# From a list scheduler to a written order with transposes on quarters of the array: a recurrent attention layer feeding a softplus layer

## The chip, the cores and the metric

The kernel runs on one core of one Trainium2 chip. The time is the device's own, in microseconds (us), for one execution. A profile is one execution recorded by the hardware profiler; its span is shorter than the timed median of the same kernel (345.8 against 349.65 us for the kernel before). TensorE is PE in the profile (PEld its weight loads), VectorE is DVE, ScalarE is ACT, GpSimd is POOL, SyncE is SP.

## The reference, cut to what matters

```python
for t in range(S):                       # S = 768, for 4 x 8 heads of 40
    y[:, :, t] = einsum('bhd,bhde->bhe', r_t, state)
    Sa = einsum('bhde,bhe->bhd', state, a_t)
    state = state * w_t - einsum('bhd,bhe->bhde', Sa, b_t) + einsum('bhd,bhe->bhde', v_t, k_t)
...                                      # y as x: 3072 tokens of 320
h = x @ w_in                             # 320 x 2048
g = maximum(h, 0) + log1p(exp(-abs(h)))
out = g @ w_out                          # 2048 x 320
```

The kernel cuts the 768 steps into 12 chunks of 64. Inside a chunk the recurrence becomes products of 64x64 (many, one per head), the inverse of a triangular matrix, and a state that passes from chunk to chunk. Two chunks share one inversion, called a window. The first two windows are inverted on VectorE, the other four on GpSimd, by an elimination of 60 steps.

## The kernel before

The program is a graph of 1839 operations. At build time a list scheduler gives each an engine, a place in the order and a PSUM bank. Each engine then takes its list in that order, waiting on semaphores (in the profile TensorE once stood 5.6 us before a product whose weights, `wout`, had not landed). Cut to what the argument touches:

```python
BLOCK, AHEAD, FETCH, BEFORE = 256, 82, 2300.0, 70    # its model of TensorE's instruction fetch
SLOW = ("h", "o", "csb")                             # dense-layer products, kept for the ends of lines
COUNT = {"tr": 8, "tot": 16, "gram": 32, ...}        # products per operation
...
def schedule(ops):
    ...
                pen = SWITCH if e == "pe" and mode is not None and o.mode != mode else 0.0
                if e == "pe":
                    pen += fetch.run(s + pen, c, 2 * COUNT[o.name])
                    if o.name in SLOW:
                        want = FILL if fetch.wants(s) else -SAVE
...
        def transpose(src, srcs, t, off):            # 72 of these, 8 products on the whole array each
            def f(e):
                for bp in X2:
                    for yy in range(H_ // 2):
                        i = T.transpose(pb(t)[:, bp, off + 128 * yy:off + 128 * yy + 128],
                                        src[:, bp, 128 * yy:128 * yy + 128], ident[:, :])
                return i
            return op(pe(8 * 56.0), srcs + ["ident"], [t], f, mode=FULL, name="tr")
...
        gexc = Ring("gexc", NEAR, [128, 2, DM], F32)  # NEAR = 4: chunk 5 takes the buffer of chunk 1
        nh = Ring("nh", NEAR, [128, 2, 512], BF)
```

Most of TensorE's products run on quarters of the array (64x64; 32 of them take 0.27 us in the trace, where a transpose of 8 products on the whole array takes 0.45). The transposes and the dense layers h and o run on the whole of it. A product is two TensorE instructions, a weight load and a matmul (8016 of each in the profile). The profile's instruction queue moved 63 packets of 16384 bytes, and 2 x 8016 instructions are 62.6 times 256. A "line" below is such a packet, or the 256 instructions that go with it.

## Time and profile before

| | before |
|---|---|
| time, 3 runs at first | 349.65 us (349.4 to 350.46) |
| span of the profile | 345.8 us |
| TensorE products, lines of 256 instructions fetched | 8016, 63 |
| first elimination step on GpSimd (the hand-over) | 114.7 us |
| end of the mask that closes GpSimd's last elimination | 294.3 us |
| from there to the end | 51.5 us |
| TensorE waits named "issue" | 4.1 us in 7 |

"GpSimd's steps" below means the time from the hand-over to the end of that mask. The three stages are a head up to the hand-over, GpSimd's chain of four inversions beside TensorE, and a tail. The page's chain of work that ended last, followed back from the end, with shares of the span by engine and then by line:

```profile
PE 47%; ACT 11%; POOL 9%; DMA 9%; SPq 9%; DVE 7%; issue 5%; ACTq 2%; DVEq 0%; POOLq 0%
PE ps L1205 12%; PE ps L1224 12%; SPq L664 8%; PE ps L730 7%; POOL mt L971 4%; DMA wout<-in_moe_w_out_dram 3%; POOL mtmp L967 3%; ACT gT L1214 3%; ACT et L1211 3%; PE ps L773 2%; DMA a_f<-in_a_dram 2%; PE ps L1073 2%; ACTq L664 2%; DMA r_f<-in_r_dram 2%; PE ps L1174 2%
```

TensorE holds 47% of the chain. "issue", time with nothing visible to wait for, has 5%. The kernel's own waits of that kind are these (engine, tile, line; total us, times, longest):

```profile
PE ps L832 <- issue: 1.7, 2, 1.0
...
PE ps L1073 <- issue: 1.4, 3, 0.7
...
PE ps L1050 <- issue: 0.5, 1, 0.5
PE ps L1174 <- issue: 0.5, 1, 0.5
```

They add up to 4.1 us.

### The profile page before, as it was taken

Reading aid. Unit: us, or ns where it says so; the run is one execution under the profiler, and the core shown is the slowest. Engines: PE = TensorE matmul, PEld = TensorE weight load, DVE = VectorE, ACT = ScalarE, POOL = GpSimd, SP = SyncE. Lnnn points to the kernel's source line nnn. Section 1 sums busy time; section 2 is a strip of 40 time slices with the busy share of each in tenths; the row PEclk is TensorE's granted clock in tenths of the full one; section 3 lists DMA queues with packets and bytes.
Section 4 is the critical chain, followed back from the end, with each engine's and each line's share of the span. In section 5 each row is a group of like instructions: output and inputs, shape, how many; then the busy total and the mean of one; then the engine's idle time right before and its main releaser. Section 6 shows DMA issues by size and latency. Waiting matters only on the chain.

```text
span 345.8 us, 17638 instructions
## 1 busy us (share of the span) xinstructions
PE 280.4 (81%) x8016; PEld 212.7 (61%) x8016; DVE 232.7 (67%) x419; ACT 210.3 (61%) x296; POOL 169.2 (49%) x309
## 2 busy tenths in 40 slices
PE   0337247688789969999799999998989899999873
PEld 0226126576567747777577776786766678777642
DVE  7729978889997746657756697585885656664201
ACT  1246704226797825877568888667687368667661
POOL 8106000001000627898888788898888888000000
PEclk9967865569999978999899999999999999999999
DMA  8999984687667565676546465430411400100101
GB/s 134 171 174 142 182 159 79 107 145 113 122 120 156 103 112 94 123 126 108 102 79 104 83 104 96 78 69 14 89 34 21 91 14 13 33 6 21 39 22 38
DMA packets 145787, 31.30 MB, mean 90 GB/s; under 512 B 140272, under 2 KB 145392, under 8 KB 145712
## 3 DMA queue, kind: packets, MB, share of 16 engines
q1 hardware_dynamic: 129504, 25.09, 42.9%
q10 hardware_dynamic: 13728, 2.46, 5.1%
q0 software_dynamic: 2480, 2.62, 4.7%
q8 instruction: 63, 1.03, 1.2%
q14 instruction: 12, 0.10, 0.1%
HBM read 28.84 MB, written 3.93 MB: 95 GB/s over the span
## 4 chain that ended last, share of the span: by engine, by line
PE 47%; ACT 11%; POOL 9%; DMA 9%; SPq 9%; DVE 7%; issue 5%; ACTq 2%; DVEq 0%; POOLq 0%
PE ps L1205 12%; PE ps L1224 12%; SPq L664 8%; PE ps L730 7%; POOL mt L971 4%; DMA wout<-in_moe_w_out_dram 3%; POOL mtmp L967 3%; ACT gT L1214 3%; ACT et L1211 3%; PE ps L773 2%; DMA a_f<-in_a_dram 2%; PE ps L1073 2%; ACTq L664 2%; DMA r_f<-in_r_dram 2%; PE ps L1174 2%
## 5 line engine op out<-in xcount | busy, mean ns | idle before, releaser
L1205 PE MATMUL ps<-xT,win 128*128 128x256 bf16 x576 | 79.9, 275 | 3.5 <-ACT et L1211 1.8
L1211 ACT ACTIVATE et<-ps 128x512 f32<-128x512 f32 x96 | 57.2, 596 | 36.3 <-PE ps L1205 35.8
L967 POOL TENSOR_TENSOR mtmp<-mt 128x30 f32<-128x30 f32 (+14 forms) x120 | 60.5, 504 | 33.0 <-DVE mt L960 24.3
L971 POOL TENSOR_TENSOR mt<-mt,mtmp 128x30 f32<-128x30 f32 (+14 forms) x120 | 66.8, 557 | 8.7
L1224 PE MATMUL ps<-wout,gT 128*128 128x320 bf16 x384 | 65.2, 302 | 5.9 <-ACT gT L1214 2.9
L1205 PEld LDWEIGHTS ps<-xT,win 128*128 128x128 bf16 x576 | 50.6, 98 | 15.9 <-ACT et L1211 6.0
L1214 ACT ACTIVATE gT<-et,hln 128x1024 bf16<-128x1024 f32 x48 | 55.2, 1151 | 1.4
L1224 PEld LDWEIGHTS ps<-wout,gT 128*128 128x128 bf16 x384 | 34.2, 98 | 20.1 <-ACT gT L1214 4.6
L1035 POOL CAST r_b<-r_f 128x640 bf16<-128x640 f32 x12 | 9.5, 789 | 44.2 <-DMA r_f<-in_r_dram 39.6
L1035 POOL CAST v_b<-v_f 128x640 bf16<-128x640 f32 x12 | 9.2, 765 | 37.0 <-DMA v_f<-in_v_dram 24.8
L1229 DVE TENSOR_TENSOR osb<-ps,csb 128x320 f32<-128x320 f32 x24 | 11.6, 484 | 20.3 <-PE ps L1224 20.1
L785 DVE TENSOR_TENSOR qt<-ps,sut 128x1024 bf16<-128x1024 f32 x12 | 14.6, 1221 | 5.6 <-PE ps L773 5.6
L814 PE MATMUL ps<-lw,nexc 64*64 64x320 bf16 x96 | 7.2, 361 | 13.8 <-ACT lw L845 13.6
L814 PE MATMUL ps<-lw,ninc 64*64 64x320 bf16 x96 | 9.8, 328 | 8.5 <-ACT ginv L862 6.2
L785 DVE TENSOR_TENSOR tak<-ps,sut 128x1024 bf16<-128x1024 f32 x12 | 14.6, 1219 | 2.8 <-PE ps L773 2.6
L785 DVE TENSOR_TENSOR pt<-ps,sut 128x1024 bf16<-128x1024 f32 x12 | 14.6, 1216 | 2.6 <-PE ps L773 2.6
L1180 DVE TENSOR_TENSOR yo<-ps,gexc 128x640 bf16<-128x640 f32 x12 | 9.9, 821 | 8.3 <-PE ps L1174 8.2
L845 ACT ACTIVATE lw<-w_f 128x1280 bf16<-128x1280 f32 x6 | 7.7, 1282 | 12.3 <-DMA w_f<-in_w_dram 12.3
L868 DVE TENSOR_TENSOR kh<-k_f,ginv 128x640 bf16<-128x640 f32 x12 | 10.9, 910 | 4.8 <-DMA k_f<-in_k_dram 4.8
L985 ACT ACTIVATE dex<-dc,blk 128x1024 bf16<-128x1024 bf16 x6 | 6.9, 1146 | 11.6 <-DVE dc L979 11.6
L866 DVE SCALAR_TENSOR_TENSOR nh<-b_f,ginv 128x640 bf16<-128x640 f32 x12 | 9.9, 825 | 5.3 <-ACT ginv L862 5.3
L862 ACT ACTIVATE ginv<-ps 128x640 f32<-128x640 f32 x12 | 8.4, 704 | 8.0 <-issue 6.8
(152 smaller groups left out, 587.9 us busy)
## 6 DMA issues: line engine op xcount, KB each, us to landing
out_dram<-osb SPq DMA_DIRECT2D x48, 80.0 KB, 2.3
b_f<-in_b_dram SPq DMA_DIRECT2D x44, 80.0 KB, 3.6
v_f<-in_v_dram SPq DMA_DIRECT2D x44, 80.0 KB, 3.3
a_f<-in_a_dram SPq DMA_DIRECT2D x44, 80.0 KB, 3.4
k_f<-in_k_dram SPq DMA_DIRECT2D x44, 80.0 KB, 3.6
r_f<-in_r_dram SPq DMA_DIRECT2D x42, 80.0 KB, 3.1
w_f<-in_w_dram SPq DMA_DIRECT2D x20, 160.0 KB, 4.2
wout<-in_moe_w_out_dram POOLq DMA_DIRECT2D x4, 320.0 KB, 10.0
```

The lines of the kernel that those rows point to most:

```text
L664: lambda e, bp=bp, x=x, q=q: queue(e).dma_start(heads(t[q:q + 64, bp, :], D_), SRC[n][2 * bp + x][:, c * L:(c + 1) * L, :].rearrange("h p ...
L730: i = T.transpose(pb(t)[:, bp, off + 128 * yy:off + 128 * yy + 128], src[:, bp, 128 * yy:128 * yy + 128], ident[:, :])
L785: lambda e: V.tensor_tensor(parity(dst), bh(pf(t), L), bc4(mask[:, :], L), ALU.mult), name="mask")
L814: i = T.matmul(pf(t)[s:s + 64, bp, 0:DM], mats[z][q:q + 64, :], heads(lwt[q:q + 64, bp, :], 2 * D_)[:, :, z * D_:z * D_ + D_], start=(z == ...
L967: lambda e, j=j, nt=nt, tv=tv: E_.tensor_tensor(tv, m[:, 0:j, j:j + 1].to_broadcast([128, j, nt]), m[:, j:j + 1, j + 1:32].to_broadcast([1 ...
L971: lambda e, j=j, tv=tv: E_.tensor_tensor(m[:, 0:j, j + 1:32], m[:, 0:j, j + 1:32], tv, ALU.add),
L1035: lambda e, dst=dst, src=src: P.tensor_copy(hd(dst), bh(src, D_)), name="cast")
L1205: i = T.matmul(one(t)[:, 256 * (q % 2):256 * (q % 2) + 256], win[:, z, q * 128:(q + 1) * 128], xT_[:, z, :], start=(z == 0), stop=(z == 2))
L1211: lambda e, q2=q2, t=t, ett=ett: A.activation(ett[:, q2 % 2, :], one(t), AF.Exp), name="exp")
L1214: lambda e, q2=q2, ett=ett: A.activation(gts[q2 // 2][0][:, :, :].rearrange("p q m -> p (q m)"), ett[:, :, :].rearrange("p q m -> p (q m)" ...
L1224: i = T.matmul(one(t)[:, 0:DM], gts[z][0][:, q % 4, bp * 128:(bp + 1) * 128], wout[:, q, :], start=(q == 0), stop=(q == NQ - 1))
L1229: lambda e, t=t, ot=ot: V.tensor_tensor(ot[:], one(t)[:, 0:DM], csb[:], ALU.add), name="oe")
```

## The change

Its author's words: an explicit order of all operations from a local search [...], and all transposes on the PE. The scheduler and its tuning tables go. Four literals take their place. Transposes get a second form on quarters, which QUARTERS asks for in 61 of 72. Cut to its core:

```diff
-BLOCK, AHEAD, FETCH, BEFORE = 256, 82, 2300.0, 70
-class Fetch: ...
-def schedule(ops): ...
+ORDER = (2, 87, 129, 48, 94, 49, ... )          # 1839 numbers
+ENGINE = ("ggggvvvvvvvvvvvvvggggvvvv ... ")     # one letter per operation
+BANK = ("24464266226226662624262624422 ... ")
+QUARTERS = (
+    "101111110011111111111111100111111111011111110011111111111111111111011100")
+def arrange(ops): ...                           # takes order, engine, bank from the four
...
+                        n = off + 64 * (4 * bp + yy)
+                        for q in (0, 64) if mode == QUAD else ():
+                            for o in (0, 64):
+                                i = T.transpose(pb(t)[o:o + 64, q // 64, n:n + 64],
+                                                src[q:q + 64, bp, 128 * yy + o:128 * yy + o + 64], eye(q))
+                        if mode == FULL:
...
-            return op(pe(8 * 56.0), srcs + ["ident"], [t], f, mode=FULL, name="tr")
+            return op(pe(8 * 56.0), srcs + ["ident"], [t], f, mode=FULL, name="tr", alt=(QUAD, 32 * 8.5, 32))
...
-                    op(pe(4 * 136.0), ["wout%d" % z, gts[z][1]], [t], fo, mode=FULL, name="o")
+                    i = op(pe(4 * 136.0), ["wout%d" % z, gts[z][1]], [t], fo, mode=FULL, name="o")
+                    i.preds.update(before[-1:])
```

A transpose on quarters is 32 products (64 instructions) where the whole-array form is 8 products (16 instructions).

## The prediction

> **What bounds the kernel now.** I read the page of the profiled execution first, then a table of busy time over four stretches that I cut at three events, then the waits, then the PE's and the GpSimd's (POOL's) timelines. The page:
>
> ```profile
> span 345.8 us, 17638 instructions
> ...
> PE 280.4 (81%) x8016; PEld 212.7 (61%) x8016; DVE 232.7 (67%) x419; ACT 210.3 (61%) x296; POOL 169.2 (49%) x309
> ...
> PE   0337247688789969999799999998989899999873
> ...
> DVE  7729978889997746657756697585885656664201
> ...
> POOL 8106000001000627898888788898888888000000
> ...
> q8 instruction: 63, 1.03, 1.2%
> ```
>
> No engine is full over the span, so the average misleads: the rows of tenths show VectorE (DVE) dense in the first third while PE is not, then PE and POOL dense together, then PE alone. The cuts: 77.3 us is where the first product of the dense layers starts, 114.7 where POOL starts its first inversion, 292 where it nears the end of its last.
>
> ```profile
> core 0: us, PE busy (x) PEld busy (x) DVE busy (x) ACT busy (x) POOL busy (x), PEclk, DMA share, GB/s
> 0.00:77.30 77.30, 38.81 (x1086) 29.49 (x1086) 59.91 (x157) 27.77 (x36) 16.71 (x42) 0.74 0.95 143
> 77.30:114.70 37.40, 32.81 (x982) 24.53 (x980) 33.75 (x58) 29.04 (x43) 2.17 (x3) 1.00 0.74 128
> 114.70:292.00 177.30, 163.90 (x4983) 126.16 (x4982) 119.08 (x175) 122.83 (x174) 147.98 (x264) 0.97 0.45 79
> 292.00:346.00 54.00, 44.89 (x994) 32.52 (x980) 19.97 (x33) 30.65 (x44) 2.35 (x1) 0.99 0.12 27
> ```
>
> Up to 114.7 us DVE is busy 59.9 + 33.8 = 93.7 us: this head is DVE's, because the two first inversions run there. It ends with a wait that names the hand-over:
>
> ```profile
> POOL mtmp L967 <- DVE mt L960: 24.3, 1, 24.3
> ...
> ACT ginv L862 <- issue: 6.8, 1, 6.8
> ...
> PE ps L705 <- DMA wout<-in_moe_w_out_dram: 5.6, 1, 5.6
> ```
>
> POOL has nothing to do for 24.3 us until DVE hands over the third matrix. From there POOL (148 of 177 us busy) and PE (164 of 177) run side by side; both are near their limit. After POOL's end 52 us of PE's work are left. The second line is ScalarE (ACT) with nothing the profile can name before it: its timeline shows five transfers issued in that hole, of 0.6 to 1.7 us each. The third is PE in program order behind a product that needs weights not yet landed.
>
> What a PE step costs I take from start-to-start distances in the warm part of the timeline:
>
> ```profile
> 207.05 0.44 PE L1082 MATMUL ps<-v_b,tak 64*64 64x40 bf16 x32
> 207.42 0.62 PE L730 MATMUL ps<-ident,kh 128*128 128x128 bf16 x8
> 207.97 0.31 PE L1073 MATMUL ps<-stateT,aT 40*64 40x40 bf16 x16
> 208.21 0.62 PE L730 MATMUL ps<-ident,v_b 128*128 128x128 bf16 x8
> ...
> 222.37 0.43 PE L1174 MATMUL ps<-kh,pt 64*64 64x40 bf16 x32
> 222.64 0.41 PE L1174 MATMUL ps<-nh,qt 64*64 64x40 bf16 x32
> ```
>
> Thirty-two products on quarters of the array take 0.27 us (222.37 to 222.64). The transpose of eight 128x128 blocks takes 0.55 here (207.42 to 207.97); where two such stand in a row (226.13, 226.59, 227.03) it is 0.45. The difference, 0.10 us, is the change between quarters and whole array; 207.05 to 207.42 shows it the other way (0.37 against 0.27).
>
> [...] the instruction queue moved 63 packets and 1.03 MB, 16 KB each, and PE's 2 x 8016 instructions are 62.6 times 256. [...] The head shows both sides: a DMA share of 0.95 to 1.09 there, and ACT idle behind its own issues. [...] a step of POOL's elimination that takes 0.65 us often takes 1.1.
>
> **The change part by part.** The arithmetic stays. (a) The list scheduler, which decided order, engine, PSUM banks at build time from a rough model, is replaced by four written-out lists. (b) A transpose may run as 32 products on quarters; the list asks for that in 61 of 72. (c) Every product of the second dense layer waits for the one before it in program order[...]. "All transposes on the PE" takes nothing away: the threshold for transposes by DMA was already 99 with 12 chunks, and the page has no transposing transfer.
>
> Counted in the two orders (before's by listing what its scheduler emits, the new one by reading the lists against the same operations):
>
> PE. Changes of mode fall from 243 to 175; with whole-array transposes the new order would have 199. So 68 x 0.10 = 6.8 us. The quarters: 61 x (0.45 - 0.27) = 11 us. Together 17.8 us of about 250 us of PE service. Against it: 24 more products and as many weight loads per transpose, 61 x 48 = 2928 instructions, 11.4 cache lines. PE's waits "issue", mostly in the middle of a run of quarter products, total about 4 us over 63 lines, up to 1.0 us each; I put the extra at 2 to 3 us (an estimate: a few of the 11 stall for most of a us). Net 15 us on PE.
>
> Head. Before the hand-over to POOL the new list has 195 operations on DVE where the old has 212. Seven fewer are small constants, about 1 us; of the evacuations, 13 to 15 of 0.33 to 0.69 us leave and 5 of 0.48 to 0.69 plus a 0.82 scaling come. Net about 8 us. The column product that waited for weights moves behind the first inversion's products. DVE idled 115 - 94 = 21 us in the head; I give it 5 back. The hand-over moves from 114.7 to about 101.
>
> POOL. Same operations plus six small constants. It took from 114.7 to 294.4 (the last mask starts at 291.5 and takes 2.8), 180 us, of which 11 are waits, the largest 7.5 for one load. I keep 170: the new list puts loads earlier but cannot shorten the chain. It ends at about 271.
>
> Tail. By PE's own steps priced as above, 43 us of PE work stood behind the last elimination step before and 49 stand there now. Before, this took 51.4 us to the end of the span. Now 49 + 4 for waits (5.3 before) + 3 for the last store = 56.
>
> Sum: 101 + 170 + 56 = 327 us of span. PE alone would allow less: 188 us of work behind the hand-over, with 20 for stalls and 3 for the last store, gives 101 + 211 = 312. So POOL is the later of the two, and of PE's 15 us perhaps half arrives. I take 325 of span, between the two but near POOL's. The timed median stands 3.9 over the profiled span before; with 3, 328.
>
> ACT issues 53 transfers instead of 26, SP 259 instead of 286. At 0.65 us that is 18 us more on ACT's sequencer, spread over the span where ACT is 61% busy; I count it as hidden, with doubt.
>
> **The rivals.** First, POOL takes all: the head does not shorten, since it is bound by loads (DMA share 0.95) and not by DVE. Then 115 + 170 + 56 = 341, plus 3: 344, within 2%. Against it: only about 1 us of DVE's named waits in the head is for loads; the longest, 5.3, is for ACT behind its issues. Second, instruction fetch and ACT's issues eat the gain: 11 lines at 1 us, and 27 issues of which a third hold up an exponential that PE waits for (9 x 0.7 us), give 328 + 9 + 6 = 343. For it: ACT's 6.8 us hole. Third, both bounds give way: a search that sees PE, POOL and the issues together may hand over at 95 and keep POOL at 165; then 95 + 165 + 54 + 3 = 317. Fourth, evacuating quarters costs DVE more, as each output row is read in runs of 64 from two banks: at 0.69 us now, twice as long would add 61 x 0.35, half of it on DVE, some 20 us in an engine with slack after the head; worth 5.
>
> **Range and chances.** 328, with 317 to 341 for 8 in 10: the low end is the third rival, the high end a head that moves by half and half of the second. The border of 2% faster is 342.7. Both independent terms, PE and head, would have to fail to miss it: faster 0.89, within 2% 0.09, slower 0.02.
>
> **What would show it right or wrong.** The instruction queue should move 74 or 75 packets. PE's idle rows should name "issue" for 5 to 9 us. The first step on POOL after the hand-over should start near 101 (95 to 107); at 113 or later the head failed. POOL's last mask should end near 271. The transposes should show 64x64 products, 32 in 0.27 us. Copies of transposes on DVE should stay at 0.69 us; over 0.9 is the fourth rival. If POOL shows gaps of several us in its chain, or ACT waits behind issues while PE waits for ACT, the fixed order is brittle and the prediction too low. If PE ends far behind POOL, with few waits between, PE was the bound and the sum of POOL's terms was the wrong sum.

The sum: 101 + 170 + 56 = 327 us of span, taken as 325 and timed as 328. The sentence on both sides of the head stands for its two readings alone. Its DMA share and the "often" of the elimination steps were misread and are put right under "Two readings" below. A "cache line" is the line of 256 instructions named above.

## The result, and the profile after

The changed kernel takes 363.66 us (median of 4, 361.93 to 365.5). The kernel before took 350.05 in the same session. The ratio of the fast runs is 1.0387, with a 95% interval of 1.0326 to 1.0447: slower by 3.9%, where I had 328 us and a chance of 0.89 for faster. Here and below a ratio is the mean time of one kernel's fast runs over that of the other's of the same rounds, so not quite the ratio of the medians quoted.

The page of the changed kernel:

```profile
span 363.7 us, 20571 instructions
...
PE 282.6 (78%) x9480; PEld 210.5 (58%) x9480; DVE 230.6 (63%) x405; ACT 215.4 (59%) x304; POOL 168.4 (46%) x315
...
PE   0453648558669798879976999888888998989895
...
DVE  6798797957666477646576586555885375754311
...
POOL 9150000300004888378898508898538778300000
...
q8 instruction: 74, 1.21, 1.4%
...
PE 55%; ACT 13%; issue 10%; DVE 8%; SPq 7%; DMA 5%; ACTq 0%; DVEq 0%
```

TensorE has 1464 products more and 11 instruction lines more (74), as foreseen. Its busy time did not fall, but a busy time sums overlapping, modelled intervals and shows neither a gain nor a loss here. What stands out is the chain: "issue" has 10% of a longer span, 36 us, where it had 5%, 17 us. The same four stretches as in the prediction, cut at this kernel's own hand-over and end of GpSimd's steps:

```profile
core 0: us, PE busy (x) PEld busy (x) DVE busy (x) ACT busy (x) POOL busy (x), PEclk, DMA share, GB/s
0.00:77.30 77.30, 35.92 (x1332) 27.39 (x1334) 61.56 (x163) 41.18 (x51) 18.45 (x48) 0.93 0.99 148
77.30:113.90 36.60, 28.13 (x1052) 21.38 (x1049) 26.05 (x35) 20.84 (x31) 2.15 (x4) 0.78 0.51 84
113.90:311.80 197.90, 173.61 (x6115) 129.91 (x6114) 123.70 (x177) 121.73 (x180) 146.93 (x264) 0.95 0.43 78
311.80:363.70 51.90, 44.94 (x986) 31.83 (x984) 19.25 (x32) 31.70 (x44) 0.82 (x1) 1.00 0.13 29
```

The hand-over is at 113.9 (before 114.7, predicted 101). GpSimd's steps last 197.9 us (before 179.6, predicted 170). The tail is 51.9 (before 51.5, predicted 56). So the loss arose between the hand-over and GpSimd's end. GpSimd is busy 147 us of it, against 150 in the kernel before: it did not work longer, it waited (32.9 us of idle time in this stretch, against 11.5 before). TensorE's waits with no named releaser:

```profile
PE ps L681 <- issue: 6.4, 7, 2.1
PE ps L629 <- issue: 4.1, 6, 1.2
PE ps L981 <- issue: 3.3, 5, 1.3
...
PE ps L1015 <- issue: 2.6, 2, 1.9
PE ps L851 <- issue: 2.3, 1, 2.3
PE ps L1082 <- issue: 2.3, 4, 1.1
```

With six smaller rows they sum to 25.2 us in 32 waits, against 4.1 in 7. One of them in TensorE's timeline (start, duration, engine, line, tiles, count, and in brackets the idle time before):

```profile
104.78 0.43 PE L629 MATMUL ps<-ident,nh 64*64 64x64 bf16 x32
105.03 0.69 PE L1058 MATMUL ps<-ident,state 40*64 40x40 bf16 x32
105.76 0.62 PE L632 MATMUL ps<-ident,ah 128*128 128x128 bf16 x8
106.35 0.41 PE L681 MATMUL ps<-rT,vT 40*64 40x64 bf16 x27
108.90 0.31 PE L681 MATMUL ps<-rT,vT 40*64 40x64 bf16 x5 [2.14 <-issue]
108.98 0.66 PE L681 MATMUL ps<-nT,aT 40*64 40x64 bf16 x32
```

The transposes on quarters do what was promised: 104.78 to 105.03, 0.25 us for 32. But a run of 32 products of the same kind (106.35) breaks after 27, TensorE waits 2.14 us, and only then come the last 5. They belong to one run of the program, with nothing between them but the end of a line.

The trace also holds the packets of the instruction queue. TensorE's instructions, counted from the trace, can be set beside these packets. In the changed kernel 33 of the 74 packets are followed, 1.9 to 3.0 us later, by a gap of over 0.1 us between matmuls that ends at position 193 or 194 of 256 by this count, 25.3 us together, as much as the "issue" waits (25.2); the middle one of them ends 2.4 us after its packet started. Gaps that recur every 256 instructions at one position are ends of lines. In the kernel before 7 of 63 packets are so followed, with 4.1 us. And from packet to packet no line took less than 3.33 us in the kernel before and 3.35 in the changed one.

### The profile page after: what moved, and what is told of

The parts are those of the page before. It is cut to its first block, busy times and chain, and to the rows that moved or that the text cites. A ratio compares the mean times of both kernels' runs of the same rounds, so it can differ in the third digit from the quotient of the medians.

```text
span 363.7 us, 20571 instructions
## 1 busy us (share of the span) xinstructions
PE 282.6 (78%) x9480; PEld 210.5 (58%) x9480; DVE 230.6 (63%) x405; ACT 215.4 (59%) x304; POOL 168.4 (46%) x315
## 4 chain that ended last, share of the span: by engine, by line
PE 55%; ACT 13%; issue 10%; DVE 8%; SPq 7%; DMA 5%; ACTq 0%; DVEq 0%
PE ps L1115 15%; PE ps L1134 11%; SPq L560 5%; PE ps L629 4%; PE ps L681 4%; ACT et L1121 4%; ACT gT L1124 3%; PE ps L981 3%; PE ps L722 2%; PE ps L1041 2%; PE ps L1082 2%; DMA w_f<-in_w_dram 2%; PE ps L1015 2%; PE ps L1058 1%; DMA a_f<-in_a_dram 1%
## 5 line engine op out<-in xcount | busy, mean ns | idle before, releaser
L1115 PE MATMUL ps<-xT,win 128*128 128x256 bf16 x576 | 83.7, 284 | 3.7 <-ACT et L1121 2.8
L875 POOL TENSOR_TENSOR mtmp<-mt 128x30 f32<-128x30 f32 (+14 forms) x120 | 61.0, 508 | 22.1 <-DVE mt L868 13.5
L1134 PE MATMUL ps<-wout,gT 128*128 128x320 bf16 x384 | 67.4, 311 | 1.5 <-DVE osb L1141 1.2
L879 POOL TENSOR_TENSOR mt<-mt,mtmp 128x30 f32<-128x30 f32 (+14 forms) x120 | 63.7, 531 | 9.0
L1134 PEld LDWEIGHTS ps<-wout,gT 128*128 128x128 bf16 x384 | 36.4, 101 | 15.9 <-DVE osb L1141 2.8
L1141 DVE TENSOR_TENSOR osb<-ps,csb 128x320 f32<-128x320 f32 x24 | 11.7, 487 | 22.7 <-PE ps L1134 21.1
L722 PE MATMUL ps<-lw,nexc 64*64 64x320 bf16 x96 | 8.8, 400 | 14.2 <-ACT lw L753 13.4
L722 PE MATMUL ps<-lw,ninc 64*64 64x320 bf16 x96 | 11.3, 372 | 6.5 <-ACT lw L753 5.0
L753 ACT ACTIVATE lw<-w_f 128x1280 bf16<-128x1280 f32 x6 | 7.6, 1264 | 13.4 <-DMA w_f<-in_w_dram 13.4
L1049 DVE TENSOR_TENSOR state<-ps,gtot 128x320 bf16<-128x320 f32 x22 | 10.0, 484 | 7.5 <-PE ps L1041 7.5
L791 DVE SCALAR_TENSOR_TENSOR mc<-ps,blk,mc 128x512 f32<-128x512 f32 x12 | 9.0, 747 | 8.6 <-ACT mc L789 8.5
L962 DVE SCALAR_TENSOR_TENSOR wexp<-ps,blk,wmask 128x512 bf16<-128x512 f32 x12 | 9.0, 747 | 7.5 <-PE ps L958 7.5
L789 ACT ACTIVATE mc<-ps,blk 128x512 f32<-128x512 f32 x12 | 8.2, 687 | 9.0 <-PE ps L681 8.8
```

Of the source, the lines that this page charges most:

```text
L722: i = T.matmul(pf(t)[s:s + 64, bp, 0:DM], mats[z][q:q + 64, :], heads(lwt[q:q + 64, bp, :], 2 * D_)[:, :, z * D_:z * D_ + D_], start=(z == ...
L875: lambda e, j=j, nt=nt, tv=tv: E_.tensor_tensor(tv, m[:, 0:j, j:j + 1].to_broadcast([128, j, nt]), m[:, j:j + 1, j + 1:32].to_broadcast([1 ...
L879: lambda e, j=j, tv=tv: E_.tensor_tensor(m[:, 0:j, j + 1:32], m[:, 0:j, j + 1:32], tv, ALU.add),
L1115: i = T.matmul(one(t)[:, 256 * (q % 2):256 * (q % 2) + 256], win[:, z, q * 128:(q + 1) * 128], xT_[:, z, :], start=(z == 0), stop=(z == 2))
L1134: i = T.matmul(one(t)[:, 0:DM], gts[z][0][:, q % 4, bp * 128:(bp + 1) * 128], wout[:, q, :], start=(q == 0), stop=(q == NQ - 1))
```

## The experiments

Sixteen runs. One table of what they left first, where "us" is the median of all executions (slow ones included, so that the ratio, of fast runs alone, is the fairer figure), "issue" is the sum of TensorE's waits of that name in the profile, and the hand-over and GpSimd's steps are read from the trace. "Ratio" is to the kernel before of the same call; the calls ran on different chips. Of each run one execution was profiled.

| run | what it is | lines | us | ratio | issue | hand-over | steps on GpSimd |
|---|---|---|---|---|---|---|---|
| before | | 63 | 350 | | 4.1 | 114.7 | 179.6 |
| after | | 74 | 363.7 | 1.039 | 25.2 | 113.9 | 197.9 |
| a_shift64 | after, 128 instructions ahead | 74 | 368.8 | none | 23.1 | 113.1 | 198.5 |
| b_shift64 | before, 128 instructions ahead | 63 | 356.2 | 1.011 | 10.6 | 116.3 | 183.1 |
| a_full | after, transposes whole | 63 | 354.7 | 1.002 | 11.7 | 115.7 | 191.0 |
| a_wide | after, 8 wide products each | 63 | 345.1 | 0.985 | 12.2 | 112.8 | 181.6 |
| a_copy | its control, 32 products each | 74 | 364.6 | 1.048 | 22.5 | 113.5 | 194.3 |
| b_quad | before's order, all on quarters | 76 | 381.0 | 1.095 | 44.0 | 122.7 | 196.4 |
| b_wide | before's order, wide products | 63 | 347.3 | 0.997 | 7.3 | 117.3 | 179.2 |
| a_mix | after, 13 on quarters | 65 | 355.3 | 1.019 | 12.8 | 117.1 | 190.0 |
| a_sp | after, ScalarE issues nothing | 74 | 364.0 | 1.043 | 22.7 | 116.8 | 193.3 |
| a_head | after, window 2 moved forward | 74 | 371.0 | 1.065 | 22.0 | 120.0 | 197.2 |
| f_head | the same, transposes whole | 63 | 363.9 | 1.046 | 6.4 | 120.8 | 204.9 |
| a_light | after, less VectorE in the head | 74 | 364.1 | 1.041 | 23.7 | 114.5 | 196.1 |
| b_light | before, less VectorE in the head | 63 | 351.1 | 1.004 | 4.7 | 116.7 | 179.9 |
| w_lessh | a_wide, less TensorE in the head | 62 | 347.5 | 0.987 | 12.4 | 111.8 | 183.1 |
| a_lessh | after, less TensorE in the head | 74 | 370.0 | 1.051 | 25.3 | 114.7 | 202.5 |
| b_lessh | before, less TensorE in the head | 62 | 352.5 | none | 6.9 | 116.0 | 180.1 |

The profiles of a_full, a_mix, b_wide, f_head and b_lessh fell in the slow state, so their last three columns are a little long, in f_head by some 6% (386.4 us where its fast runs took 363.5). "none" stands where too few fast runs were left for a ratio.

### Is it where a line ends?

My first theory came from the scheduler of the kernel before. It keeps slow dense-layer products (0.65 us for an h of 12 instructions in the trace) for the last 82 instructions of a line, where its model of the fetch has them hide the wait for the next. If the written order lives from that, moving every line's end must ruin it. 64 quarter products (128 instructions, 0.5 us) ahead of TensorE's first product do that:

```diff
+        pad = Op({"pe": 0.0}, [], [], lambda e: [
+            T.matmul(psf[0:64, 0, 0:64], ident[0:64, 0:64], ident[0:64, 0:64], start=True, stop=True)
+            for _ in range(64)][-1], name="tr")
+        order.insert(next(i for i, o in enumerate(order) if o.eng == "pe"), pad)
```

> The changed kernel with 64 extra quarter products (0.5 us) on TensorE before its first real product, while TensorE waits for loads; nothing else moves, but every later TensorE instruction sits 128 further on in its line of 256. Theory (instruction fetch: TensorE stops at the end of a line of 256 until the next line has come, about 2.4 us after its transfer starts, and the written order only hides that where slow dense-layer products stand ahead of the line's end): the slow products now stand in the middle of lines, so most of 75 ends cost 1 to 2 us; from the order with back-to-back costs I work out about 95 us more of stalls than at the old phase; with part of it hidden in other waits, 410 to 470 us. Rival (the loss lies in the order of loads and of GpSimd's work, fetch is a side effect): 364 plus 0.5 us, within 1%.

> The same 64 extra quarter products ahead of the kernel before. Fetch theory: it too lives from its phase (slow products at line ends); the same working gives 50 us more stalls, less than for the changed kernel as it has 11 fewer lines and more full-array work; 375 to 410 us. Rival: 350 plus 0.5 us.

The changed kernel took 365.6 us in its one fast run (the other was slow, 372.0), the kernel before 356.2, 1.1% above its neighbours (ratio 1.003 to 1.0192). The waits did not grow in the changed kernel (25.2 to 23.1) and grew by 6.5 us in the kernel before. The theory of the line's end had asked for 50 to 100 us and falls. The rival (fetch is a side effect) was nearer, yet the waits at ends of lines stay.

What fits is simpler: not where the line ends but how much time its 256 instructions hold. I priced every operation by its warm cost in the trace of the kernel before (0.27 us for 32 quarter products, 0.45 for a whole transpose, 0.65 for an h, 0.54 for an o, 0.1 for a change of mode) and added them up line by line. A mean line holds 4.2 us in the kernel before and 3.2 in the changed one, and a line does not follow another in less than 3.33 us there, 3.35 in the changed kernel. Summing what each line lacks to 3.45 us gives, as an estimate, 16 us for the kernel before, 38 for the changed one and 16 for the changed one with whole transposes. A shift by 128 instructions changes these sums by 1 to 3 us. These sums are rough: a recount from the traces, with costs read there, gives 3.9 and 3.1 us for a mean line, 16, 49 and 22 us for the three sums, and 4 us for a shift. The direction is the same, the sizes are not. I call this theory A.

### Quarters or order?

```diff
-    "101111110011111111111111100111111111011111110011111111111111111111011100")
+QUARTERS = "0" * 72
```

> The changed kernel with all 72 transposes on the whole array (no quarters); order, engines and banks stay. 2928 TensorE instructions fewer, so 63 lines instead of 74, but the ends of the lines leave the slow products. Fetch theory: 11 us more of transposes, 2.4 us of changes of mode, and some 27 us more of stalls by the same working, since the phase is lost: 385 to 410 us, slower than the changed kernel. Rival 1 (quarters cost more than they give, apart from phase): faster than 364. Rival 2 (loads and GpSimd's order): 364 to 378, the 13 us of dearer transposes at most.

The expectation was still that of the fallen theory, and it was wrong: 354.7 us (fast runs 352.7 to 354.7), 9 us faster than the changed kernel and equal to the kernel before (ratio 1.0024, 0.9956 to 1.0092). This settles two things. In this order the quarters cost 9 us by the medians and some 13 us by the two ratios, where theory A prices 13.4 us less work against 22 us more shortfall. And the new order, with whole transposes, gives nothing measurable over the old.

### Instructions, or something else about quarters?

To keep the quarters and take away only the instructions, each quarter transpose becomes 8 products of 64x256 instead of 32 of 64x64. This copies instead of transposing, so the result is wrong. Mode, order, columns streamed and the evacuations stay.

```diff
-                        for q in (0, 64) if mode == QUAD else ():
-                            for o in (0, 64):
-                                i = T.transpose(pb(t)[o:o + 64, q // 64, n:n + 64], ...)
+                        for q in (0, 64) if mode == QUAD and yy % 2 == 0 else ():
+                            i = T.matmul(psf[32 * yy:32 * yy + 64, t.bank + q // 64, off // 2:off // 2 + 256],
+                                         eye(q), src[q:q + 64, bp, 128 * yy:128 * yy + 256], start=True, stop=True)
```

> Wrong result on purpose. The changed kernel, but each of its 61 quarter transposes is 8 products of 64x64 by 64x256 against the identity (a copy, no transpose) in place of 32 of 64x64 by 64x64: same mode, same order, same columns streamed, 48 TensorE instructions fewer each, 63 lines in all as before. Theory A (a line of 256 TensorE instructions takes at least about 3.4 us to come, whatever stands at its end, so instructions cost and not their phase): per line I compare the content priced at warm costs with 3.45 us; the shortfall sums to 38 us for the changed kernel, 20 here, 16 for all transposes whole, 16 for the kernel before. So about 18 us faster than the changed kernel: 343 to 350 us. Rival B (quarters are slow for another reason[...]): stays at 360 to 364. Rival C (order of loads and GpSimd's work): stays at 360 to 364 too.

```profile
span 344.9 us, 17643 instructions
...
PE 271.4 (79%) x8016; PEld 195.9 (57%) x8016; DVE 230.0 (67%) x405; ACT 214.9 (62%) x304; POOL 170.0 (49%) x315
...
q8 instruction: 63, 1.03, 1.2%
```

345.1 us, 18.6 below the changed kernel, where 18 were expected. Against the kernel before the ratio is 0.985 with an interval of 0.9693 to 1.0012, so it is not shown to be faster than that. The control makes the same copy into the same places from 32 products of 64 columns:

```diff
+                            for j in range(4):
+                                i = T.matmul(... off // 2 + 64 * j ..., src[..., 128 * yy + 64 * j:...], ...)
```

> Wrong result on purpose, the control of the run with 8 wide products: the same copy against the identity into the same places, but as 32 products of 64x64 by 64x64, so 9480 products and 74 lines as in the changed kernel. Theory A (lines): 361 to 366 us, as the changed kernel, against 345 with the wide ones. Rival (the wide run was fast because its data are wrong, or because a copy is cheaper than a transpose): 345 to 350.

```profile
span 359.9 us, 20571 instructions
...
PE 279.0 (78%) x9480; PEld 209.3 (58%) x9480; DVE 231.1 (64%) x405; ACT 214.9 (60%) x304; POOL 168.3 (47%) x315
...
q8 instruction: 74, 1.21, 1.4%
```

364.6 us. The two differ only in how many instructions carry the same columns, and 1464 products make 19.5 us (22 by the ratios to the kernel before of each call). So it is neither the wrong data nor the copy. It is not the granted clock: at a clock near 0.90 a_wide took 342.2 us and a_copy 361.6. Nor are the many products slower in themselves, for 8 wide ones take 0.25 us in a_wide's timeline, as 32 narrow ones did above:

```profile
200.44 0.41 PE L627 MATMUL ps<-nh,ident 64*64 64x256 bf16 x8
200.69 0.41 PE L627 MATMUL ps<-ah,ident 64*64 64x256 bf16 x8
```

In the two profiled executions the spans differ by 15.0 us and the gaps at ends of lines (counted as above) by 10.4 us, 23.3 against 12.9. That the cost comes with the instructions is shown. That a late TensorE then makes GpSimd wait for the remainder is the likely reading, since GpSimd's steps are 12.7 us longer in a_copy, but no run isolates it. The same question in the other order puts all 72 on quarters in the unchanged order of the kernel before, then in the wide form:

> The order, engines and banks of the kernel before, all 72 transposes on quarters. Theory A: TensorE's own work falls by 15.6 us (265 to 249 us by the pricing) and 13 lines are added; the shortfall goes from 16 to 49 us; net 17 us slower, of which most arrives, as TensorE stands beside GpSimd: 360 to 370 us. Rival (quarters gain, the new order loses): 335 to 345 us.

> Wrong result on purpose. The order of the kernel before with all 72 transposes as 8 wide products on quarters: quarter mode without the instructions. Theory A by line pricing: TensorE's work 265 to 249, shortfall 16 to 20, net 11 us less on TensorE, part of which GpSimd's chain (180 us from 115) keeps: 340 to 348 us. If the new order is worth something apart from fetch, this run must be slower than the 345 us of the wide form in the new order; if the order is worth nothing, equal or faster.

```profile
span 379.1 us, 21094 instructions
...
PE 283.4 (75%) x9744; PEld 208.0 (55%) x9744; DVE 234.3 (62%) x419; ACT 212.8 (56%) x296; POOL 168.9 (45%) x309
...
q8 instruction: 76, 1.25, 1.4%
...
PE 57%; issue 15%; DVE 12%; ACT 9%; DMA 3%; SPq 2%; ACTq 1%; DVEq 0%
```

b_quad has 76 lines, 44 us of "issue" waits, 15% of its chain named "issue", and takes 381 us. That is 31 us above before, and more than the 17 that the line pricing gave: the sign and the cause hold, the size is off (48 of its 76 packets are followed by a gap at the line's end, 46.8 us together). Two things beyond the pricing are visible: the hand-over is 8 us later, and the tail is 60.0 us instead of 51.5. b_wide takes 347.3 (ratio 0.997). It passes the comparison with the reference although it transposes nothing, so the comparison is not sensitive here. With 63 lines, 11 us cheaper on TensorE by the pricing, it gains nothing measurable: GpSimd's steps still take 179 us. It fits that TensorE's relief is hidden behind GpSimd in the kernel before, but no run tests that apart.

The pair also prices the order. On quarters the new order is 17 us better than the old (364 against 381), a part of it because b_quad puts 72 transposes on quarters and not 61. In the wide form the two are 345.1 and 347.3, from different calls and with overlapping intervals. If the search fitted its order to quarters, what it won there was less than their instructions cost.

### Few quarters

> The changed kernel with quarters on 13 transposes only, chosen by the line pricing of theory A where a line holds enough slow work. Theory A: 4 us less of work and shortfall than with all whole (355 in the last call), 14 less than the changed kernel: 347 to 353 us. Rival (quarters cost by number, apart from lines): about 355 plus 13/61 of 9 us, 356 to 358.

```diff
+    "001000000000000000000000100000011000000010000000000000000011011100001110")
```

A miss: 355.3 us (ratio 1.019), no better than with all whole (1.002), though well below the changed kernel. The pricing of lines ranks whole kernels but is too coarse to pick 13 transposes.

### ScalarE's issues

```diff
-        o.eng = names[ENGINE[n]]
+        o.eng = "sp" if o.dma and ENGINE[n] == "a" else names[ENGINE[n]]
```

> The changed kernel with its 53 transfers that ScalarE issues given to SyncE, at the same places of the order. My second rival in the prediction (ScalarE's issues hold up exponentials that TensorE waits for) expects 5 us or more faster. Theory A: within 1.5% of 364, slower if anything, since SyncE's queue gets longer and stands behind its stores.

364.0 us, unchanged within the noise. Where ScalarE's 53 issues stand is no measurable part of the loss.

### The head

The prediction had the hand-over at 101. It is at 112.8 even in a_wide, so instruction fetch alone does not explain it. In the changed kernel's trace the last operations before it are these on VectorE and GpSimd:

```profile
102.33 0.82 DVE L1088 TENSOR_TENSOR yo<-ps,gexc 128x640 bf16<-128x640 f32 x1
103.06 0.82 DVE L774 SCALAR_TENSOR_TENSOR nh<-b_f,ginv 128x640 bf16<-128x640 f32 x1
103.98 0.82 DVE L772 TENSOR_TENSOR ah<-a_f,gexc 128x640 bf16<-128x640 f32 x1
...
111.20 1.93 DVE L868 STREAM_TRANSPOSE mt<-mc 128x1024 f32<-128x1024 f32 x1
```

```profile
113.19 0.72 POOL L943 CAST r_b<-r_f 128x640 bf16<-128x640 f32 x1 [5.74 <-DMA r_f<-in_r_dram]
113.88 0.24 POOL L875 TENSOR_TENSOR mtmp<-mt 128x30 f32<-128x30 f32 x1
```

yo is chunk 1's output (102.33). nh and ah are chunk 5's and take chunk 1's buffers. The third matrix is handed over at 113.1, and at the same time (113.19) GpSimd's cast of r_b stands in its list ahead of the first step and has just got its load. Two chains end within 0.1 us. The first test gives chunk 5 buffers of its own for gexc and nh and moves its 13 operations forward in the written order:

```diff
+        fifth = {n: (sb(n + "4", [128, 2, m], d), n + ".4") for n, m, d in (("gexc", DM, F32), ("nh", 512, BF))}
-        pt = Ring("pt", 2, [128, 2, H_, L], BF)
+        pt = Ring("pt", 1, [128, 2, H_, L], BF)
-    ORDER: 704, 709, 705, 708, 713, 714, 711, 712, 715, 716, 717, 719, 718 at places 503 to 530
+    ORDER: the same at places 452 to 522
```

> The changed kernel with a fifth buffer for gexc and nh of chunk 5 (memory from pt, one buffer instead of two) and its 13 operations up to the hand-over of the third matrix moved forward in the list by about 9 us. Theory H: in the new order the hand-over to GpSimd is not VectorE's count of operations but chunk 1's output product, after which alone chunk 5 may overwrite gexc and nh (102 us in the trace), plus 11 us of chain; freed of that, GpSimd starts at 103 to 107 instead of 113.9. Time: 355 to 361 us if GpSimd's chain then sets the end; 362 to 366 if TensorE's lines do, since nothing is taken from TensorE (theory A). Rival: the start stays at 112 or later, as loads or VectorE hold it.

> The same with all 72 transposes whole (63 lines). Theory H: GpSimd starts at 105 to 109 instead of 115.7. With TensorE relieved of 11 lines, more of it should arrive than with quarters: 345 to 351 us against 354.7 with the late start. Rival: no gain, 353 to 357.

Both fail: the hand-over comes later (120.0 and 120.8), and the times are 371.0 and 363.9. VectorE's timeline of a_head shows why:

```profile
104.57 0.82 DVE L686 SCALAR_TENSOR_TENSOR nh<-b_f,ginv 128x640 bf16<-128x640 f32 x1
105.95 0.69 DVE L358 COPY nT<-ps 128x1024 bf16<-128x1024 bf16 x1 [0.56 <-PE ps L541]
106.56 0.81 DVE L684 TENSOR_TENSOR ah<-a_f,gexc 128x640 bf16<-128x640 f32 x1
114.32 0.75 DVE L703 SCALAR_TENSOR_TENSOR mc<-ps,blk,mc 128x512 f32<-128x512 f32 x1 [6.95 <-ACT mc L701]
114.99 0.88 DVE L961 TENSOR_TENSOR state<-ps,gtot 128x320 bf16<-128x320 f32 x2
115.79 1.92 DVE L780 STREAM_TRANSPOSE mt<-mc 128x1024 f32<-128x1024 f32 x1
```

nh, at 104.57, and ah, at 106.56, directly follow other work of VectorE. Then the mask step at 114.32 waits 6.95 us for ScalarE, which had itself waited 6.4 us for TensorE, whose list had other products in between. The matrix is ready at 117.7, and GpSimd's cast of r_b, next in its list, waits for a product of TensorE and holds the first step to 120.0 (118.2 and 120.8 in f_head). My hand-made order was bad in its own way, and pt had lost a buffer, so these two runs do not say whether the shared buffers hold the head. They do show how much a few misplaced operations cost when each engine runs a list.

Two more pairs take work out of the head and leave all orders alone. Six masks of chunks 0 and 1 become constants (0.48 us in place of 1.22 each, wrong):

```diff
-               lambda e: V.tensor_tensor(parity(dst), bh(pf(t), L), bc4(mask[:, :], L), ALU.mult), name="mask")
+               lambda e, light=g.tag[0] in ("before", "after") and g.tag[1] < 2: V.memset(dst, 0.0) if light else
+               V.tensor_tensor(parity(dst), bh(pf(t), L), bc4(mask[:, :], L), ALU.mult), name="mask")
```

> Wrong result on purpose. The changed kernel with six masks of chunks 0 and 1 on VectorE (1.22 us each, all due before the hand-over) replaced by constants of about 0.3 us: some 5.5 us less work on VectorE ahead of the hand-over. The prediction's step (the head is VectorE's count of work): GpSimd starts 5 us earlier, near 108.5. Theory P (the path into the hand-over runs through TensorE and ScalarE, and twice over through a load that GpSimd's cast waits for; VectorE has slack): 112 to 114. Time 360 to 366.

> Wrong result on purpose. The same six masks of the kernel before replaced by constants. The prediction's step: GpSimd starts near 109 instead of 114.7, and the time falls by about as much, 344 to 347. Theory P: in the kernel before too the path back from the hand-over runs through TensorE from 102 to 109 and ScalarE from 91 to 102; start 113 to 116, time within 1%.

The first 114.7 us of b_light:

```profile
0.00:114.70 114.70, 69.18 (x1985) 51.85 (x1986) 86.51 (x213) 55.18 (x77) 19.07 (x45) 0.84 0.89 137
```

VectorE is busy 86.5 us there. By the prediction's count it was 93.7 in the kernel before; the six masks account for 4.4 us of that. The hand-over is at 116.7, not earlier. In the changed kernel it is at 114.5. The times, 351.1 and 364.1 us, are those of the kernels that they derive from. So VectorE's amount of work does not bound the head in either kernel, as far as one profile of each can show. The last three take 4 of 6 products out of each h of chunk 0 (also wrong):

```diff
-                        for z in range(3):
+                        for z in range(3) if c else (2,):
```

> Wrong result on purpose. The wide form of the changed kernel (no extra lines), with 2 of 6 products in each of the eight first-layer steps of chunk 0; seven of them stand before the hand-over: about 3.5 us less of TensorE's work there. Theory T (the head of the new order is TensorE's in-order work on chunks 0 and 1, through which chunk 1's product and with it buffers for chunk 5 come late): GpSimd starts near 109.5 instead of 112.8. Rival: 112 to 114, the start hangs on something else (loads, ScalarE).

> The same in the changed kernel. Theory T alone would say 110.5 instead of 113.9; theory A takes part of it back, as lines in the head lose slow work (the ends of lines stall longer): 111 to 113.5. Rival: 113 to 115.

> The same in the kernel before, where the eight steps stand between 77 and 98 us and the last 12 us before the hand-over ran through ScalarE and TensorE: 111.5 to 114 if TensorE's order counts there too; 114 to 116 if not.

111.8, 114.7 and 116.0: at most 1 us of 3.5 arrives. So TensorE's amount of work is not shown to be the head's bound either. The changed kernel even took 370.0 us here. Theory A allows that sign, since slow products fill lines, but its head also had a granted clock of 0.55 in that run, so I don't rest on it.

What sets the hand-over stays open. The traces show one difference between the orders: in every run on the order of the kernel before, GpSimd stands idle 23 to 27 us until the matrix comes. In the new order its cast of r_b stands before the first step and ends within 1 us of the matrix in most runs, and 1.6 to 2.7 us after it in a_full, a_mix, a_head and f_head. TensorE's clock from 77 to 113 us is 0.78 in the changed kernel against 1.00 before, but the clock does not rank the hand-overs: a_shift64 had 0.75, 0.59 and 0.74 in three thirds of its head and handed over at 113.1, while the changed kernel had 1.00, 0.86 and 0.78 and did so at 113.9.

## Why the prediction was wrong

It was wrong in the direction, and the step that failed there is the term "I put the extra at 2 to 3 us (an estimate: a few of the 11 stall for most of a us)", with its sum "Net 15 us on PE". It measured 19.5 us, about half of the 37 us by which the span exceeds the sum of 327 below. A second step makes the other half: "this head is DVE's", with the hand-over at 101, and GpSimd's 170 after it.

- **Instruction count.** "The instruction queue should move 74 or 75 packets": 74.
- **Their cost.** "PE's idle rows should name 'issue' for 5 to 9 us": 25.2. The same columns carried by 1464 products more cost 19.5 us (a_copy less a_wide). I took the 4 us of the kernel before, divided by 63 lines, as the price of a line. But that kernel's lines hold 4.2 us of work on average, and only 7 of its 63 packets were followed by a gap at the line's end. Moving 61 transposes to quarters takes 11 us out and puts 11 lines in, and the lines fall to 3.2 us, below the 3.35 us that the quickest line took from packet to packet. Quarter products alone would use up 256 instructions in 1.1 us, as an estimate (128 products, 32 in 0.27 us). I had the second rival, "11 lines at 1 us", and its sign was right; I priced 11 new lines only, where 26 more packets than before are followed by a gap (33 against 7). The kernel before held a warning that I passed over: its scheduler's model of the fetch charges 2300 ns for a line, asked for 82 instructions ahead. Those two are its constants; what the trace of the changed kernel shows is that the middle gap ended 2.4 us after its packet started.
- **Quarters.** "The transposes should show 64x64 products, 32 in 0.27 us": 0.25. The service time was right. What it gains without the instructions is small at best: a_wide's ratio to the kernel before is 0.985, not clear of 1.
- **Copies.** The fourth rival (evacuation of quarters) is refuted for VectorE. Its copy of aT in the changed kernel and in the one before, with count, total and mean ns:

```profile
L450 DVE COPY aT<-ps 128x1024 bf16<-128x1024 bf16 x7 | 4.8, 686 | 0.8 <-PE ps L629 0.8
```

```profile
L549 DVE COPY aT<-ps 128x1024 bf16<-128x1024 bf16 x9 | 6.2, 685 | 2.1 <-PE ps L730 2.0
```

- **The head.** "The hand-over moves from 114.7 to about 101" failed on its own: 113.9, and 112.8 without the cost of instructions. I read VectorE's 94 busy us of 115 as the bound. Its busy time ahead of the hand-over did fall, from 93.7 to 87.6 us (my "about 8" stood at the upper end of its own parts), and the hand-over did not follow. Nor did it in b_light, where VectorE was busy 7 us less. The first rival's figure (115) was right; its reason, loads, is one of two chains that end together and is not shown to be the cause.
- **GpSimd.** "I keep 170" was a hope: 197.9 came, 181.6 in a_wide. Its busy time did not grow (147 against 150), so the rest is waits. In the changed kernel they are for matrices and loads that come late (totals over the whole run):

```profile
POOL r_b L943 <- DMA r_f<-in_r_dram: 64.6, 6, 24.8
POOL v_b L943 <- DMA v_f<-in_v_dram: 37.2, 6, 19.4
POOL mtmp L875 <- DVE mt L868: 13.5, 3, 7.1
```

  The largest waits of the first two rows lie ahead of the hand-over. Of the 32.9 us of waits after it, 13.5 are for mt, the later matrices, and 16.8 for loads. In a_wide the waits after the hand-over come to 14.3 us. So most of the difference goes with the instructions; that TensorE's stalled stream makes matrices and loads late is argued, not shown.
- **Tail.** 56 predicted, 51.9 measured, 50.5 in a_wide. TensorE's share of it was a little overpriced.
- **ScalarE's issues**, "hidden, with doubt": hidden (a_sp).
- **Two readings.** The DMA share in the head goes up to 1.14 (20 to 40 us), not 1.09. And elimination steps on GpSimd do not "often" take 1.1 us: 14 of 240 took over 0.3 us more than their like, up to 1.16 us. Each of the 14 ran beside VectorE's nh, ah or kh.

Put together: 101 + 170 + 56 = 327 was to come. a_wide, which is the change as I priced it, gives 112.8 + 181.6 + 50.5 = 344.9 us of span: 11.8 more in the head, 11.6 more on GpSimd, 5.5 less in the tail. The other 18.8 us of span come with the instructions. What holds the first 18 is not found. With the fetch priced right my sum would have given 346, still 18 short of the 363.7 of the profile, and the call would have been "within 2%".

None of the runs gives a correct kernel that beats the one before: a_wide does not transpose, and the correct ones with whole or few quarter transposes are equal to it or slower.

## What to carry to other kernels

Price a TensorE change by its instructions as well as its columns: add up the work that each 256 instructions hold, and see where that falls under the shortest line-to-line time that the trace shows. Here that was 3.35 us, a mean line of the changed kernel held 3.2 us, and TensorE waited 25.2 us in 32 "issue" waits although 32 of its products took only 0.25 us. Such a sum gave the sign here, not the size (17 us where b_quad lost 31), and could not pick 13 good transposes. A cheap way to test it is to carry the same columns in fewer, wider products and let the result be wrong. And a dense engine is not a bound until work taken off it moves the event that it is said to hold.
